# Weight-gradient products over 448 features as three full contractions and one half, with the halves of two output tiles on two row groups of the array

## The chip, the cores and the metric

The kernel runs on one core of one Trainium2 chip. The metric is device time in microseconds (us). Times from several runs are medians. TensorE multiplies and leaves its sums in PSUM, a memory that the kernel uses in banks of 512 columns. DVE (VectorE) and ACT (ScalarE) do elementwise work and copy the finished sums out of PSUM, POOL (GpSimd) does small copies, and SP issues the DMA transfers. PE is TensorE's row in the profile and PEld its weight loads, which put a stationary tile into the array; the granted clock is the share of its full clock that TensorE got.

## The reference, cut to what matters

The reference is forward and backward of a small network on one sequence of 2048 positions and 448 features: a spectral mixer (two-dimensional FFT, pointwise product with `A_w`, inverse FFT), then a token MLP of width 1792, each behind LayerNorms, with residuals. Eight outputs come back. Two of them matter here, the gradients of the MLP weights:

```
grad B_w1 (2048 x 1792) = LayerNorm(h)  (2048 x 448)  times  du        (448 x 1792)
grad B_w2 (1792 x 2048) = gelu(u)       (1792 x 448)  times  grad_out^T (448 x 2048)
```

Both contract over 448 features. No matmul in these kernels contracts more than 128 rows at a time, and 448 is 3.5 times 128.

## The kernel before

It contracts 448 as four times 112 (`DC = 112`). Activations are kept in blocks of 128 columns of which 112 are used, so that one DMA transpose makes four stationary tiles. The products are a generator. Each `yield` is one filler step. The other stages of the backward pass call `fill(n)` to put products between their own matmuls.

```python
RESH_LAG = 1.1
N_FILL_B = (16, 16, 40, 8, 32, 12)      # [2] before, [3] in, [4] after the spectral stage; [5] per inverse row

    rS = region("rS", 2 * NFB * 256)    # 7168 columns, scratch of the spectral stage
    ...
    def mm(out, lhsT, rhs, start, stop):
        nc.tensor.matmul(out, lhsT=lhsT, rhs=rhs, start=start, stop=stop)
    ...
    def gw_gen(n, rhs, width, store):
        for j in range(n):
            st = ahead.pop(0)                       # a transposed tile, 4 x 112 rows
            o = ost.next()
            for c in range(4):
                w = min(512, width - 512 * c)
                pw = ps_mm()                        # one of four PSUM banks
                for k in range(4):
                    mm(pw[:, 0:w], lhsT=st[0:DC, k, :], rhs=rhs(c, k), start=(k == 0), stop=(k == 3))
                    if k == 3:
                        evac(out=o[:, c * 512:c * 512 + w], in_=pw[:, 0:w])
                        if c == 3:
                            st_load()               # ask for a later transposed tile
                            defer(1.5, lambda j=j, o=o: store(j, o), o)
                    yield
    ...
    # the spectral stage on DVE, for two groups at a time
    ve.tensor_tensor(out=p1, in0=xc, in1=wr, op=ALU.mult)
    ve.tensor_tensor(out=p2, in0=xc, in1=wi, op=ALU.mult)
    ve.tensor_tensor(out=y[:, :, 1, :], in0=p1[:, :, 0, :], in1=p2[:, :, 1, :], ...)
    ve.tensor_tensor(out=y[:, :, 0, :], in0=p1[:, :, 1, :], in1=p2[:, :, 0, :], ...)
    # p1, p2, y and the emptied PSUM of the stage all lie in rS
```

Of the kernel before, what the change touches and what calls it, by code (L numbers as in the profile page):

```python
# [13 lines left out]
ALU = mybir.AluOpType  # L14
# [104 lines left out]
def kernel(  # L119
# [34 lines left out]
    def region(name, n):  # L154
        return mem.tile([P, n], BF16, name=name)
# [72 lines left out]
    r3 = region("r3", NG * 2 * KW)  # L228
    rS = region("rS", 2 * NFB * 256)
    rO = region("rO", 3 * S)  # L230
    rX = region("rX", NG * 2 * KW)
    r452 = region("r452", 8 * 452)
    rAT = region("rAT", 2 * 4 * P)
    rst = region("rst", 3 * 4 * P)
    r448 = region("r448", 8 * D)
# [21 lines left out]
    go_tp = cut(rC, 0, NT, D)  # L257
    dgu = cut(rD, 0, NFB, 4, P)[:, :, :, 0:DC]
    goT = cut(rG, 0, 4, S)
# [57 lines left out]
    gp_.memset(gtail, 0.0)  # L317
    nc.sync.dma_start(out=gtail[:, 0:DC], in_=grad_out[0][S - 16:S, 3 * DC:D])

# [462 lines left out]
    def dg_gen():  # L782
        for j in range(NFB):
            wT = w2Ts.pop(0)
            pg = ps_mm()
            for t in range(NT):
                mm(pg[:, 0:D], lhsT=wT[:, t, :], rhs=go_tp[:, t, :], start=(t == 0), stop=(t == NT - 1))
                if t == NT - 1:
                    evac(out=dgu[:, j, :, :], in_=v4(pg[:, 0:D]))
                    if w2T_ring.i >= cap[0]:  # L790
                        held_w2.append(load_w2T)
                    else:
                        load_w2T()
                yield
# [119 lines left out]
    hn = xn  # L914
    hln = cut(rB, 0, NT, 4, P)[:, :, :, 0:DC]

# [25 lines left out]
    def norm_h(t, on_act=False):  # L942
        if on_act:
            sc.activation(out=hln[:, t, :, :], in_=v4(hn[:, t, :]), func=ACT.Identity,
                          scale=rstd_h[:, t:t + 1], bias=nmr_h[:, t:t + 1])
        else:
            ve.tensor_scalar(out=hln[:, t, :, :], in0=v4(hn[:, t, :]), scalar1=nmean_h[:, t:t + 1],
                             scalar2=rstd_h[:, t:t + 1], op0=ALU.add, op1=ALU.mult)

    w2c_ring = Ring([cut(r, o, NFB, 256) for r, o in ((rS, 0), (rS, NFB * 256), (r452, 0), (rA, 0), (rA, NFB * 256), (r2, 0))])  # L950
# [18 lines left out]

    g_ = cut(rE, 0, NFB, 4, P)[:, :, :, 0:DC]  # L970
    gel = [ring(rG, i * 4 * 896, 4, 2, D) for i in range(2)]
# [27 lines left out]
    for jp in range(NFB // 2):  # L999
# [7 lines left out]
        for jj, ta, tb in spans:  # L1007
            fb = f0 + jj
            pu = pus[jj]
            for t in range(ta, tb):  # L1010
                mm(pu[:, 0:D], lhsT=w1c[:, t, jj * P:(jj + 1) * P], rhs=hln[:, t, :, :],
                                 start=(t == 0), stop=(t == NT - 1))
            if tb == NT:
                sc.activation(out=uf[:, jj, :], in_=pu[:, 0:D], func=ACT.Identity, bias=b1col[:, fb:fb + 1], scale=1.0)
        if jp + 3 < NFB // 2:
            w1cs.append(load_w1c(jp + 3))
        for fn in after_u.get(jp, ()):
            fn()
        gj = g_[:, f0:f0 + 2, :, :]

        def q4(ap):
            return ap.rearrange("p j (b c) -> p j b c", b=4)
        sc.activation(out=x2, in_=uf, func=ACT.Square)
# [4 lines left out]
        ve.tensor_scalar(out=hh, in0=z, scalar1=0.5, scalar2=0.5, op0=ALU.mult, op1=ALU.add)  # L1028
        ve.tensor_tensor(out=gj, in0=q4(uf), in1=q4(hh), op=ALU.mult)
        d = Later(ve, om_ops) if jp >= NFB // 2 - 2 else ve  # L1030
        d.tensor_scalar(out=om, in0=z, scalar1=-1.0, scalar2=1.0, op0=ALU.mult, op1=ALU.add)
        d.tensor_tensor(out=om, in0=om, in1=x2, op=ALU.mult)
        d.tensor_tensor(out=q4(om), in0=q4(om), in1=gj, op=ALU.mult)
        d.tensor_tensor(out=om, in0=om, in1=hh, op=ALU.add)
        for jj in range(2):
            d.tensor_tensor_reduce(out=dgu[:, f0 + jj, :, :], in0=dgu[:, f0 + jj, :, :], in1=v4(om[:, jj, :]), scale=1.0,
                                    scalar=0.0, op0=ALU.mult, op1=ALU.add, accum_out=gb1[:, f0 + jj:f0 + jj + 1])
    du = dgu
    gp_.memset(gb1b, 0.0)
# [6 lines left out]

    def load_goT(c):
        if c < 3:
            nc.sync.dma_start_transpose(out=goT[:, c, :], in_=grad_out[0][:, c * DC:c * DC + P])
            return  # L1050
        g0 = grad_out[0]
        nc.sync.dma_start_transpose(out=goT[:, 3, 0:S - 16],
                                    in_=bass.AP(g0.tensor, g0.offset + 3 * DC, [[D, S - 16], [1, P]]))
        nc.sync.dma_start_transpose(out=goT[:, 3, S - 16:S], in_=gtail)


    def y_head(t, lo_, hi_, py):
        for j in range(lo_, hi_):
            mm(py[:, 0:D], lhsT=w2cs[t // 2][:, j, (t % 2) * P:(t % 2 + 1) * P], rhs=g_[:, j, :, :],
                             start=(j == 0), stop=(j == NFB - 1))  # L1060
# [32 lines left out]
    ve.tensor_copy(out=gb2b[:], in_=gb2[:])  # L1093
    zero = mem.tile([P, P - DC], BF16, name="zero")
    gp_.tensor_scalar(out=zero[:], in0=gb2b[:], scalar1=0.0, scalar2=None, op0=ALU.mult)
    for reg, n in ((rE, NFB), (rD, NFB), (rB, NT)):
        gp_.tensor_copy(out=cut(reg, 0, n, 4, P)[:, :, :, DC:P].rearrange("p a b c -> p (a b) c"),
                        in_=zero[:, None, :].broadcast_to([P, 4 * n, P - DC]))
    defer(4.0, lambda: nc.sync.dma_start(out=out_7.rearrange("(p t) -> p t", t=NT), in_=gb2b[:]))
# [10 lines left out]
    def ln_bwd(t, i, ps, pscale, nrm, m2scale, rstd, resid, out):  # L1110
        pb, junk, tmp = m448.next(), m448.next(), m448.next()
        four = len(nrm.shape) == 3
        w = v4 if four else (lambda a: a)
        ms, m1, m2 = (lcol[:, i, k:k + 1] for k in range(3))
        sc.activation(out=pb, in_=ps, func=ACT.Identity, scale=pscale, accum_out=ms)
        ve.tensor_tensor_reduce(out=w(junk), in0=w(pb), in1=nrm, scale=m2scale, scalar=0.0,
                                op0=ALU.mult, op1=ALU.add, accum_out=m2)
        ve.tensor_scalar(out=m1, in0=ms, scalar1=1.0 / D, scalar2=None, op0=ALU.mult)
        ve.tensor_scalar(out=w(tmp), in0=nrm, scalar1=m2, scalar2=m1, op0=ALU.mult, op1=ALU.add)
        ve.tensor_tensor(out=pb, in0=pb, in1=tmp, op=ALU.subtract)  # L1120
        ve.scalar_tensor_tensor(out=out, in0=pb, scalar=rstd, in1=resid, op0=ALU.mult, op1=ALU.add)

    LAG = 3
    st_ring = ring(rst, 0, 3, 4, P)
    order = [(rE, j) for j in range(NFB)] + [(rB, t) for t in range(NT)]
    ahead = []

    def st_load():
        if order:
            reg, j = order.pop(0)  # L1130
            st = st_ring.next()
            nc.sync.dma_start_transpose(out=st, in_=reg[:, j * 512:(j + 1) * 512])
            ahead.append(st)
# [9 lines left out]
    for t in range(NT):  # L1143
        wT = w1Ts.pop(0)
        pdh = ps_mm()
        for j in range(NFB):
            mm(pdh[:, 0:D], lhsT=wT[:, j, :], rhs=du[:, j, :, :], start=(j == 0), stop=(j == NFB - 1))
        if t + 4 < NT:
            load_w1T(t + 4)
        ln_bwd(t, t, pdh[:, 0:D], 1.0, hln[:, t, :, :], (1.0 + LN_EPS) / D, rstd_h[:, t:t + 1], go_pt[:, t, :], dh[:, t, :])  # L1150
        if t % 2:
            fold_prep(dh, t // 2)
        if t >= NT - 3:
            st_load()
# [22 lines left out]

    ost = ring(rO, 0, 3, S)
    o4 = out_4.rearrange("(p t) f -> p t f", t=NT)

    def gw_gen(n, rhs, width, store):
        for j in range(n):
            st = ahead.pop(0)
            o = ost.next()
            for c in range(4):
                w = min(512, width - 512 * c)
                pw = ps_mm()
                for k in range(4):
                    mm(pw[:, 0:w], lhsT=st[0:DC, k, :], rhs=rhs(c, k), start=(k == 0), stop=(k == 3))
                    if k == 3:  # L1190
                        evac(out=o[:, c * 512:c * 512 + w], in_=pw[:, 0:w])
                        if c == 3:
                            st_load()
                            defer(1.5, lambda j=j, o=o: store(j, o), o)
                    yield

    pending.append(gw_gen(NFB, lambda c, k: goT[0:DC, k, c * 512:(c + 1) * 512], S,
                          lambda j, o: nc.sync.dma_start(out=out_6[j * P:(j + 1) * P, :], in_=o)))
    pending.append(gw_gen(NT, lambda c, k: du_t[0:DC, 4 * c:min(NFB, 4 * c + 4), k, :], F,
                          lambda t, o: nc.sync.dma_start(out=o4[:, t, :], in_=o[:, 0:F])))  # L1200
    nc.sync.dma_start(out=rC[:, 0:NG * 2 * KW], in_=w_d[:])
# [52 lines left out]
```

## Time and profile before

| | before |
|---|---|
| time, median | 388.18 us (386.99 to 388.26, 3 runs) |
| profiled execution | 386.6 us, granted clock 0.999 |
| product matmuls | 480 of 112 rows, 416 of 512 columns and 64 of 256 |

The busy time of each engine, from the first part of the profile page of the kernel before:

```profile
PE 353.7 (91%) x2089; PEld 192.4 (50%) x2089; DVE 286.2 (74%) x738; ACT 207.0 (54%) x437; POOL 24.0 (6%) x96
```

The table of windows gives the busy time by stage. The stretches below are the forward spectral stage (52 to 87.5), then in the backward pass the row transforms among which the products begin (244.1), the spectral stage, the filler after it, the inverse rows, and what follows the last inverse row. The columns are the stretch, its length, busy us (and instructions) of PE, PEld, DVE, ACT and POOL, the granted clock, the mean busy share of the DMA engines, and GB/s.

```profile
52.10:87.50 35.40, 30.22 (x184) 16.73 (x182) 29.17 (x67) 24.03 (x48) 0.96 (x3) 1.00 0.76 149
244.10:261.30 17.20, 15.69 (x92) 8.19 (x90) 9.49 (x19) 7.46 (x14) 0.00 (x0) 1.00 0.91 242
261.30:309.50 48.20, 46.14 (x233) 22.43 (x232) 45.38 (x94) 25.86 (x53) 0.00 (x0) 1.00 0.74 201
309.50:317.90 8.40, 8.40 (x43) 4.05 (x42) 3.56 (x6) 3.49 (x6) 0.00 (x0) 1.00 0.84 233
317.90:375.70 57.80, 52.69 (x321) 28.88 (x320) 43.02 (x114) 38.74 (x85) 0.00 (x0) 1.00 0.94 214
375.70:386.60 10.90, 6.84 (x38) 3.52 (x36) 5.39 (x12) 4.00 (x9) 0.00 (x0) 0.96 0.50 191
```

In the spectral stage TensorE and DVE are both nearly full. In the inverse rows TensorE idles 57.8 - 52.7 = 5.1 us, while the DMA engines are 94% busy. The list of waits for the inverse rows (who waited for what: us in total, times, longest) says what for:

```profile
DVE r L78 <- DMA out_dram<-r: 9.2, 5, 3.1
PE ps_mm L213 <- DVE rO L78: 3.6, 3, 2.1
PE ps_mm L213 <- DMA rst<-rB: 1.5, 1, 1.5
```

DVE wants to reuse a buffer whose row of `grad A_x` has not yet landed in DRAM. It is then late with emptying a PSUM bank, and TensorE waits for that. The timeline of TensorE shows the pace (start, length, operation, how many) and the end of the kernel:

```profile
268.17 1.89 PE L213 MATMUL ps_mm<-rG,rst 112*128 112x512 bf16 x8
...
372.53 2.75 PE L213 MATMUL ps_mm<-r,rst 112*128 112x512 bf16 x12
375.12 0.92 PE L213 MATMUL ps_ff<-csI,rAT 113*128 113x448 bf16 x4
375.88 6.66 PE L213 MATMUL ps_mm<-r,rst 112*128 112x256 bf16 x36
```

A run of eight lasts 1.89 us because the last one's pipeline is counted in; the starts are 0.216 us apart. After the last inverse row (375.12) 36 product matmuls are left, and they run while DVE and ACT finish the last LayerNorm.

### The profile page before, as it was taken

The numbers are of one execution on the slowest core, as the hardware profiler recorded it, in microseconds if no ns is written. First come the engines' busy times: TensorE is split into PE (matmuls) and PEld (weight loads), VectorE is DVE, ScalarE is ACT, GpSimd is POOL, SyncE is SP. The second block draws the span as 40 slices with busy tenths as digits, with TensorE's granted clock in tenths as the row PEclk, the third lists the DMA queues.
The fourth block names the chain that finished last, engine by engine and source line by source line (L and its number), as shares of the span: only waits on it lengthen the run. The fifth ranks groups of instructions, "written<-read, shape, count | busy, mean of one in ns | idle before, by whom it ended". The sixth has DMA issues, their size and how long they took to land.

```text
span 386.6 us, 6229 instructions
## 1 busy us (share of the span) xinstructions
PE 353.7 (91%) x2089; PEld 192.4 (50%) x2089; DVE 286.2 (74%) x738; ACT 207.0 (54%) x437; POOL 24.0 (6%) x96
## 2 busy tenths in 40 slices
PE   0888998789999999999999999899999899779995
PEld 0454655345645555555555666545544355445552
DVE  8999649973867887762269878738999945589694
ACT  4576646665966535233213444435545547557862
POOL 8600000000210000000030000000000000000000
PEclk9999999999999999999999999999999999999999
DMA  8999899537999999987857794595679889986994
GB/s 219 299 169 251 143 189 185 127 96 258 292 302 341 325 293 233 232 245 176 210 122 156 166 191 98 171 279 166 191 219 209 212 245 286 209 182 177 218 222 166
DMA packets 146248, 81.85 MB, mean 212 GB/s; under 512 B 97448, under 2 KB 140456, under 8 KB 145832
## 3 DMA queue, kind: packets, MB, share of 16 engines
q1 hardware_dynamic: 146216, 81.46, 86.6%
q8 instruction: 16, 0.26, 0.3%
q14 instruction: 16, 0.13, 0.1%
HBM read 27.56 MB, written 23.89 MB: 133 GB/s over the span
## 4 chain that ended last, share of the span: by engine, by line
PE 58%; DVE 26%; DMA 6%; ACT 4%; issue 4%; SPq 1%; POOL 0%; DVEq 0%; ACTq 0%; POOLq 0%
PE ps_mm L213 50%; DVE rS L78 10%; PE ps_ff L213 8%; DMA out_dram<-r 6%; DVE r L78 5%; DVE stats L78 2%; DVE rO L78 2%; ACT rO L78 2%; DVE rG L78 1%; DVE rX L78 1%; ACT rS L78 1%; DVE rC L78 1%; DVE rA L78 1%; DVE rD L78 1%; ACT csI L78 1%
## 5 line engine op out<-in xcount | busy, mean ns | idle before, releaser
L213 PEld LDWEIGHTS <-r 128*128 128x128 bf16 (+1 forms) x568 | 54.4, 105 | 43.6 <-issue 1.6
L213 PEld LDWEIGHTS <-rst 112*128 112x128 bf16 x480 | 45.9, 97 | 50.5 <-issue 5.7
L213 PE MATMUL ps_mm<-r,rst 112*128 112x512 bf16 (+1 forms) x256 | 52.0, 352 | 5.1 <-DVE rO L78 3.6
L213 PE MATMUL ps_mm<-rG,rst 112*128 112x512 bf16 x224 | 53.1, 378 | 0.0
L78 ACT CAST rO<-ps_mm 128x512 bf16<-128x512 f32 (+1 forms) x63 | 35.6, 572 | 31.9 <-PE ps_mm L213 30.4
L213 PEld LDWEIGHTS <-rS 128*128 128x128 bf16 (+1 forms) x368 | 32.0, 98 | 36.6 <-DVE rS L78 9.6
L78 DVE CAST rO<-ps_mm 128x512 bf16<-128x512 f32 (+1 forms) x57 | 35.1, 629 | 14.7 <-PE ps_mm L213 13.5
L213 PE MATMUL ps_mm<-rD,r 128*128 128x448 bf16 x224 | 44.5, 352 | 0.0
L213 PE MATMUL ps_mm<-rC,rE 128*128 128x448 bf16 x144 | 35.6, 367 | 1.5 <-DMA rE<-in_B_w_dram 1.5
L213 PE MATMUL ps_mm<-rB,r 128*128 128x448 bf16 x160 | 31.1, 352 | 0.1
L78 ACT CAST r<-ps_ff 128x452 bf16<-128x452 f32 x49 | 26.4, 540 | 6.5 <-PE ps_ff L213 6.5
L78 DVE SCALAR_TENSOR_TENSOR r<-ps_mm,b2col,r 128x448 bf16<-128x448 f32 x16 | 10.9, 683 | 20.2 <-PE ps_mm L213 18.2
L213 PE MATMUL ps_ff<-csI,rAT 113*128 113x448 bf16 x108 | 24.9, 353 | 0.4 <-ACT rAT L78 0.2
L78 ACT ACTIVATE r<-ps_mm 128x448 bf16<-128x448 f32 x16 | 8.7, 544 | 30.7 <-PE ps_mm L213 30.7
L78 ACT ACTIVATE r<-rC 128x448 bf16<-128x448 bf16 x16 | 9.1, 571 | 26.7 <-DMA out_dram<-r 13.5
L78 ACT ACTIVATE rS<-rS 128x452 bf16<-128x452 bf16 x16 | 9.3, 580 | 23.6 <-DVE rS L78 23.6
L213 PE MATMUL ps_mm<-rE,rS 128*128 128x448 bf16 x112 | 21.5, 352 | 0.0
L78 ACT ACTIVATE rG<-rG 128x896 bf16<-128x896 bf16 x14 | 13.3, 950 | 14.9 <-DVE rG L78 14.7
L213 PEld LDWEIGHTS <-rO 128*128 128x128 bf16 (+1 forms) x165 | 15.6, 98 | 10.6 <-ACT rO L78 0.2
L213 PEld LDWEIGHTS <-rE 128*128 128x128 bf16 x144 | 13.9, 101 | 12.1 <-DMA rE<-in_B_w_dram 1.9
L213 PE MATMUL ps_mm<-rC,rO 128*128 128x448 bf16 x80 | 18.9, 352 | 0.0
L78 ACT CAST rS<-ps_ff 128x512 bf16<-128x512 f32 x27 | 15.7, 586 | 5.4 <-PE ps_ff L213 5.4
(160 smaller groups left out, 573.0 us busy)
## 6 DMA issues: line engine op xcount, KB each, us to landing
out_dram<-rO SPq DMA_DIRECT2D x14, 512.0 KB
out_dram<-rO SPq DMA_DIRECT2D x16, 448.0 KB
r<-in_B_w_dram SPq DMA_DIRECT2D x5, 1024.0 KB
r<-r SPq DMA_DIRECT2D x16, 226.0 KB
r<-r SPq DMA_DIRECT2D x32, 113.0 KB
rS<-in_B_w_dram SPq DMA_DIRECT2D x4, 896.0 KB
out_dram<-r SPq DMA_DIRECT2D x32, 112.0 KB
rO<-in_B_w_dram SPq DMA_DIRECT2D x2, 1024.0 KB
```

What stands on the lines that cost most here:

```text
L78: fn(**kw)
L213: nc.tensor.matmul(out, lhsT=lhsT, rhs=rhs, start=start, stop=stop)
```

## The change

The intent is to save one eighth of the product matmuls' time. 448 rows become three full tiles of 128 and one half of 64. Two output tiles are made together. Their halves stand in rows 0 to 63 and 64 to 127 of one stationary block, so they can run on two row groups of the array at once. The Trainium skill ("TensorE: Matmul & The Clock Gate", Part 3) describes such tiles as running concurrently. To make one transposed tile of seven blocks, the last 64 features of the odd tile are copied in front of it, and the moving operands carry their last 64 features twice. The 112-of-128 layouts become dense ones.

```diff
-    rS = region("rS", 2 * NFB * 256)
+    rS = region("rS", 7232)
...
-    st_ring = ring(rst, 0, 3, 4, P)
-    order = [(rE, j) for j in range(NFB)] + [(rB, t) for t in range(NT)]
+    st_ring = Ring(ring(rst, 0, 2, 7, P).views + [cut(rS, 6336, 7, P)])
+    fold_ring.views.pop()
+    order = [(rE, j) for j in range(NFB // 2)] + [(rB, t) for t in range(NT // 2)]
...
-            nc.sync.dma_start_transpose(out=st, in_=reg[:, j * 512:(j + 1) * 512])
+            nc.sync.dma_start_transpose(out=st, in_=reg[:, j * 1024 + 64:j * 1024 + 960])
...
+        for u in range(n // 2):
+            def whole(pw, w, c, i, k, start, stop):
+                mm(pw[i][:, 0:w], lhsT=st[:, 4 * i + k, :], rhs=rhs(c, k, 0, P), start=start, stop=stop)
+            def parts(pw, w, c, start):
+                for i in range(2):
+                    mm(pw[i][:, 0:w], lhsT=st[64 * i:64 * i + 64, 3, :], rhs=rhs(c, 3, 64 * i, 64 * i + 64),
+                       start=start, stop=not start)
...
+            for c in range(0, 4, 2):
...
+                pw = [ps_mm(), ps_mm()]
+                for i in range(2):
+                    for k in range(3):
+                        whole(pw, 512, c, i, k, k == 0, False)
+                        yield
...
+                pv = [ps_mm(), ps_mm()]
+                parts(pw, 512, c, False)          # ends the two sums of chunk c
+                parts(pv, w, c + 1, True)         # begins the two sums of chunk c + 1
+                for i in range(2):
+                    out(pw, 512, c, i)
+                yield
+                yield
+                for i in range(2):
+                    for k in range(3):
+                        whole(pv, w, c + 1, i, k, False, k == 2)
+                        if k == 2:
+                            out(pv, w, c + 1, i)  # each half row is stored by itself
+                        yield
```

Cut here: POOL's zero-fill of the padding, which goes, the small POOL copies of 64 columns that replace it, the store buffers (six half rows instead of three rows), the number of transposed loads asked for in advance (two instead of three), and the renaming of layouts. The fill counts `N_FILL_B` stay as they are.

More of the change, by code (lines that the diff above doesn't have):

```diff
@@ L233 @@
     rAT = region("rAT", 2 * 4 * P)
-    rst = region("rst", 3 * 4 * P)
+    rst = region("rst", 2 * 7 * P)
     r448 = region("r448", 8 * D)
@@ L257 @@
     go_tp = cut(rC, 0, NT, D)
-    dgu = cut(rD, 0, NFB, 4, P)[:, :, :, 0:DC]
+    dgu = cut(rD, 0, NFB, 512)[:, :, 0:D]
     goT = cut(rG, 0, 4, S)
@@ L317 @@
     gp_.memset(gtail, 0.0)
-    nc.sync.dma_start(out=gtail[:, 0:DC], in_=grad_out[0][S - 16:S, 3 * DC:D])
+    nc.sync.dma_start(out=gtail[:, 0:64], in_=grad_out[0][S - 16:S, 3 * P:D])
     s896, s128, s2048 = _sin_scale(896), _sin_scale(128), _sin_scale(2048)
@@ L788, in dg_gen @@
                 if t == NT - 1:
-                    evac(out=dgu[:, j, :, :], in_=v4(pg[:, 0:D]))
+                    evac(out=dgu[:, j, :], in_=pg[:, 0:D])
                     if w2T_ring.i >= cap[0]:
@@ L914 @@
     hn = xn
-    hln = cut(rB, 0, NT, 4, P)[:, :, :, 0:DC]
+    hln = cut(rB, 0, NT, 512)[:, :, 64:512]
     hsum = mvh[:, :, 0]
@@ L943, in norm_h @@
         if on_act:
-            sc.activation(out=hln[:, t, :, :], in_=v4(hn[:, t, :]), func=ACT.Identity,
+            sc.activation(out=hln[:, t, :], in_=hn[:, t, :], func=ACT.Identity,
                           scale=rstd_h[:, t:t + 1], bias=nmr_h[:, t:t + 1])
         else:
-            ve.tensor_scalar(out=hln[:, t, :, :], in0=v4(hn[:, t, :]), scalar1=nmean_h[:, t:t + 1],
+            ve.tensor_scalar(out=hln[:, t, :], in0=hn[:, t, :], scalar1=nmean_h[:, t:t + 1],
                              scalar2=rstd_h[:, t:t + 1], op0=ALU.add, op1=ALU.mult)
+        if t % 2:
+            gp_.tensor_copy(out=rB[:, 512 * t:512 * t + 64], in_=rB[:, 512 * t + 448:512 * t + 512])
     w2c_ring = Ring([cut(r, o, NFB, 256) for r, o in ((rS, 0), (rS, NFB * 256), (r452, 0), (rA, 0), (rA, NFB * 256), (r2, 0))])
@@ L968 @@
     nc.sync.dma_start(out=h_d.rearrange("(p t) d -> p t d", t=NT), in_=hn)
-    g_ = cut(rE, 0, NFB, 4, P)[:, :, :, 0:DC]
+    g_ = cut(rE, 0, NFB, 512)[:, :, 64:512]
     gel = [ring(rG, i * 4 * 896, 4, 2, D) for i in range(2)]
@@ L1010 @@
             for t in range(ta, tb):
-                mm(pu[:, 0:D], lhsT=w1c[:, t, jj * P:(jj + 1) * P], rhs=hln[:, t, :, :],
+                mm(pu[:, 0:D], lhsT=w1c[:, t, jj * P:(jj + 1) * P], rhs=hln[:, t, :],
                                  start=(t == 0), stop=(t == NT - 1))
@@ L1018 @@
             fn()
-        gj = g_[:, f0:f0 + 2, :, :]
-        def q4(ap):
-            return ap.rearrange("p j (b c) -> p j b c", b=4)
+        gj = g_[:, f0:f0 + 2, :]
         sc.activation(out=x2, in_=uf, func=ACT.Square)
@@ L1028 @@
         ve.tensor_scalar(out=hh, in0=z, scalar1=0.5, scalar2=0.5, op0=ALU.mult, op1=ALU.add)
-        ve.tensor_tensor(out=gj, in0=q4(uf), in1=q4(hh), op=ALU.mult)
+        ve.tensor_tensor(out=gj, in0=uf, in1=hh, op=ALU.mult)
+        o1 = 512 * (f0 + 1)
+        gp_.tensor_copy(out=rE[:, o1:o1 + 64], in_=rE[:, o1 + 448:o1 + 512])
         d = Later(ve, om_ops) if jp >= NFB // 2 - 2 else ve
@@ L1032 @@
         d.tensor_tensor(out=om, in0=om, in1=x2, op=ALU.mult)
-        d.tensor_tensor(out=q4(om), in0=q4(om), in1=gj, op=ALU.mult)
+        d.tensor_tensor(out=om, in0=om, in1=gj, op=ALU.mult)
         d.tensor_tensor(out=om, in0=om, in1=hh, op=ALU.add)
         for jj in range(2):
-            d.tensor_tensor_reduce(out=dgu[:, f0 + jj, :, :], in0=dgu[:, f0 + jj, :, :], in1=v4(om[:, jj, :]), scale=1.0,
+            d.tensor_tensor_reduce(out=dgu[:, f0 + jj, :], in0=dgu[:, f0 + jj, :], in1=om[:, jj, :], scale=1.0,
                                     scalar=0.0, op0=ALU.mult, op1=ALU.add, accum_out=gb1[:, f0 + jj:f0 + jj + 1])
+            o1 = 512 * (f0 + jj)
+            dup = Later(gp_, om_ops) if d is not ve else gp_
+            dup.tensor_copy(out=rD[:, o1 + 448:o1 + 512], in_=rD[:, o1 + 384:o1 + 448])
     du = dgu
@@ L1047, in load_goT @@
     def load_goT(c):
+        g0 = grad_out[0]
         if c < 3:
-            nc.sync.dma_start_transpose(out=goT[:, c, :], in_=grad_out[0][:, c * DC:c * DC + P])
+            nc.sync.dma_start_transpose(out=goT[:, c, :], in_=g0[:, c * P:(c + 1) * P])
             return
-        g0 = grad_out[0]
         nc.sync.dma_start_transpose(out=goT[:, 3, 0:S - 16],
-                                    in_=bass.AP(g0.tensor, g0.offset + 3 * DC, [[D, S - 16], [1, P]]))
+                                    in_=bass.AP(g0.tensor, g0.offset + 3 * P, [[D, S - 16], [1, P]]))
         nc.sync.dma_start_transpose(out=goT[:, 3, S - 16:S], in_=gtail)
+        nc.sync.dma_start(out=goT[64:P, 3, :], in_=goT[0:64, 3, :])
     def y_head(t, lo_, hi_, py):
         for j in range(lo_, hi_):
-            mm(py[:, 0:D], lhsT=w2cs[t // 2][:, j, (t % 2) * P:(t % 2 + 1) * P], rhs=g_[:, j, :, :],
+            mm(py[:, 0:D], lhsT=w2cs[t // 2][:, j, (t % 2) * P:(t % 2 + 1) * P], rhs=g_[:, j, :],
                              start=(j == 0), stop=(j == NFB - 1))
@@ L1093 @@
     ve.tensor_copy(out=gb2b[:], in_=gb2[:])
-    zero = mem.tile([P, P - DC], BF16, name="zero")
-    gp_.tensor_scalar(out=zero[:], in0=gb2b[:], scalar1=0.0, scalar2=None, op0=ALU.mult)
-    for reg, n in ((rE, NFB), (rD, NFB), (rB, NT)):
-        gp_.tensor_copy(out=cut(reg, 0, n, 4, P)[:, :, :, DC:P].rearrange("p a b c -> p (a b) c"),
-                        in_=zero[:, None, :].broadcast_to([P, 4 * n, P - DC]))
     defer(4.0, lambda: nc.sync.dma_start(out=out_7.rearrange("(p t) -> p t", t=NT), in_=gb2b[:]))
@@ L1111, in ln_bwd @@
         pb, junk, tmp = m448.next(), m448.next(), m448.next()
-        four = len(nrm.shape) == 3
-        w = v4 if four else (lambda a: a)
         ms, m1, m2 = (lcol[:, i, k:k + 1] for k in range(3))
         sc.activation(out=pb, in_=ps, func=ACT.Identity, scale=pscale, accum_out=ms)
-        ve.tensor_tensor_reduce(out=w(junk), in0=w(pb), in1=nrm, scale=m2scale, scalar=0.0,
+        ve.tensor_tensor_reduce(out=junk, in0=pb, in1=nrm, scale=m2scale, scalar=0.0,
                                 op0=ALU.mult, op1=ALU.add, accum_out=m2)
         ve.tensor_scalar(out=m1, in0=ms, scalar1=1.0 / D, scalar2=None, op0=ALU.mult)
-        ve.tensor_scalar(out=w(tmp), in0=nrm, scalar1=m2, scalar2=m1, op0=ALU.mult, op1=ALU.add)
+        ve.tensor_scalar(out=tmp, in0=nrm, scalar1=m2, scalar2=m1, op0=ALU.mult, op1=ALU.add)
         ve.tensor_tensor(out=pb, in0=pb, in1=tmp, op=ALU.subtract)
@@ L1146 @@
         for j in range(NFB):
-            mm(pdh[:, 0:D], lhsT=wT[:, j, :], rhs=du[:, j, :, :], start=(j == 0), stop=(j == NFB - 1))
+            mm(pdh[:, 0:D], lhsT=wT[:, j, :], rhs=du[:, j, :], start=(j == 0), stop=(j == NFB - 1))
         if t + 4 < NT:
             load_w1T(t + 4)
-        ln_bwd(t, t, pdh[:, 0:D], 1.0, hln[:, t, :, :], (1.0 + LN_EPS) / D, rstd_h[:, t:t + 1], go_pt[:, t, :], dh[:, t, :])
+        ln_bwd(t, t, pdh[:, 0:D], 1.0, hln[:, t, :], (1.0 + LN_EPS) / D, rstd_h[:, t:t + 1], go_pt[:, t, :], dh[:, t, :])
         if t % 2:
             fold_prep(dh, t // 2)
-        if t >= NT - 3:
+        if t >= NT - 2:
             st_load()
@@ L1176, in bwd_mult @@
         return y
-    ost = ring(rO, 0, 3, S)
+    ost = ring(rO, 0, 6, S // 2)
     o4 = out_4.rearrange("(p t) f -> p t f", t=NT)
     def gw_gen(n, rhs, width, store):
-        for j in range(n):
+        for u in range(n // 2):
             st = ahead.pop(0)
-            o = ost.next()
-            for c in range(4):
-                w = min(512, width - 512 * c)
-                pw = ps_mm()
-                for k in range(4):
-                    mm(pw[:, 0:w], lhsT=st[0:DC, k, :], rhs=rhs(c, k), start=(k == 0), stop=(k == 3))
-                    if k == 3:
-                        evac(out=o[:, c * 512:c * 512 + w], in_=pw[:, 0:w])
-                        if c == 3:
-                            st_load()
-                            defer(1.5, lambda j=j, o=o: store(j, o), o)
-                    yield
@@ L1197 @@
-    pending.append(gw_gen(NFB, lambda c, k: goT[0:DC, k, c * 512:(c + 1) * 512], S,
-                          lambda j, o: nc.sync.dma_start(out=out_6[j * P:(j + 1) * P, :], in_=o)))
-    pending.append(gw_gen(NT, lambda c, k: du_t[0:DC, 4 * c:min(NFB, 4 * c + 4), k, :], F,
-                          lambda t, o: nc.sync.dma_start(out=o4[:, t, :], in_=o[:, 0:F])))
+            def whole(pw, w, c, i, k, start, stop):
+                mm(pw[i][:, 0:w], lhsT=st[:, 4 * i + k, :], rhs=rhs(c, k, 0, P), start=start, stop=stop)
@@ new lines, in parts, with out @@
+            def parts(pw, w, c, start):
+                for i in range(2):
+                    mm(pw[i][:, 0:w], lhsT=st[64 * i:64 * i + 64, 3, :], rhs=rhs(c, 3, 64 * i, 64 * i + 64),
+                       start=start, stop=not start)
+            def out(pw, w, c, i):
+                o = os_[i]
+                x = c % 2 * 512
+                evac(out=o[:, x:x + w], in_=pw[i][:, 0:w])
+                if x:
+                    if c == 3 and i:
+                        st_load()
+                    defer(1.5, lambda j=2 * u + i: store(j, 512 * (c - 1), x + w, o), o)
@@ new lines, in gw_gen @@
+            for c in range(0, 4, 2):
+                os_ = [ost.next(), ost.next()]
+                pw = [ps_mm(), ps_mm()]
[3 more added lines that the diff above has]
+                        yield
+                w = min(512, width - 512 * (c + 1))
+                pv = [ps_mm(), ps_mm()]
[11 more added lines that the diff above has]
+                        yield
@@ L1201 @@
+    pending.append(gw_gen(NFB, lambda c, k, a, b: goT[a:b, k, c * 512:(c + 1) * 512], S,
+                          lambda j, a, n, o: nc.sync.dma_start(out=out_6[j * P:(j + 1) * P, a:a + n], in_=o[:, 0:n])))
+    pending.append(gw_gen(NT, lambda c, k, a, b: du_t[a:b, 4 * c:min(NFB, 4 * c + 4), k, :], F,
+                          lambda t, a, n, o: nc.sync.dma_start(out=o4[:, t, a:a + n], in_=o[:, 0:n])))
     nc.sync.dma_start(out=rC[:, 0:NG * 2 * KW], in_=w_d[:])
```

## The prediction

> **What bounds it now.** The profile's first part has TensorE busy 91% of a 386.6 us span (DVE 74%, ACT 54%), at full clock. The products that change start at 244 us. The table of windows gives the stages. The spectral stage, 265 to 308 us, is bound by DVE and TensorE together: DVE is busy 9.7 to 9.8 of every 10 us from 270 to 310; an iteration takes 5.0 to 5.6 us. The inverse-row stage, 318 to 376 us, is bound by TensorE at 3.15 us an iteration, with some 5 us of gaps from 331 to 348 us, where DVE waited for output transfers (9.2 us in 5 waits) and TensorE for a transposed tile and for evictions. At the end, 36 product matmuls (375.9 to 382.5 us) hide the last LayerNorm work; then 4 us of eviction and store.
>
> **What is removed.** 480 product matmuls of 112 rows become 360 of 128 rows and 120 of 64. The timeline spaces 512-column matmuls by 0.216 us. If the halves run in pairs at once, 60 slots go: 12.1 us, counting the 256-column ones. The zero-fill on POOL goes too (3.6 us, hidden).
>
> **What is added.** 30 blocks of four half matmuls between full-array ones, so 60 switches of array mode. The Trainium skill, "TensorEngine Tiling (Array Packing)", Key Properties, says that a change of mode drains the array and that tiles work in parallel; no trace here has shown either. My estimate from this trace: a matmul lasts 379 ns against 216 spacing, so a drain costs up to 163 ns, and the weight load after it (98 ns) may be partly uncovered: 80 to 250 ns a switch. Block: 0.43 + 0.16 to 0.50 us, against 0.86 now. Net TensorE saving: 12.1 minus 5 to 15; I take 4. Evictions stay at 120. POOL's small copies lie off the chain; dense instead of 4x112 layouts gain nothing. Stores are twice as many, half as large; transposed loads move 13,440 instead of 15,360 columns.
>
> **How much is critical.** In the spectral stage DVE's own work does not shrink, and 16 fill steps now carry 18.3 matmuls, so it gets perhaps 1 to 4 us longer: accumulators finish two at a time, and a bank is wanted again after 6 matmuls rather than 12, so TensorE may wait for DVE's evictions. More products are then done there, and the gain appears in the inverse rows. The filler has 420 steps instead of 480, with unchanged fill counts: 168 steps remain for the inverse rows at 12 each, so the last two iterations have no filler. They run at the speed of ACT and DVE (about 2.3 us of DVE each), and the last LayerNorm tail and store are exposed: about 4 us lost against the present ending. Sum: -4 + 4, and 1 us less from lighter transfers and a smaller last store.
>
> **Prediction.** 387.0 us, 380 to 395 eight times in ten. Faster by over 2%: 0.10; within 2%: 0.80; slower by over 2%: 0.10.
>
> **What would show it.** Concurrency: start times of two halves within some 60 ns; a block of four taking 0.6 to 0.9 us. Spectral stage: 43 us or longer. End: two inverse-row iterations without product matmuls, TensorE mostly idle in the last 8 to 10 us. Everything before 244 us unchanged within 1 us.
>
> **What would make it wrong.** Halves that do not overlap: 7 to 15 us slower. Switches that cost almost nothing: up to 8 us faster. PSUM banks freed late, or transposed tiles of 896 columns, asked for one pair ahead, arriving late between 320 and 350 us: several us slower.

## The result and the profile after

The changed kernel took 382.92 us (median of 4 runs, 382.45 to 383.19) against 387.80 us for the kernel before in the same rounds. The ratio is 0.9875, with a 95% interval of 0.9854 to 0.9897. A ratio is the mean time of one kernel's fast runs over that of the other's of the same rounds, so it is not quite the ratio of the medians. The 1.25% are clear of the noise. Medians of different jobs come from different chips, so the comparisons below go by ratios.

The busy times of the changed kernel, from its profile page (span 381.4 us):

```profile
PE 348.6 (91%) x2089; PEld 181.7 (48%) x2089; DVE 284.7 (75%) x736; ACT 207.4 (54%) x439; POOL 29.0 (8%) x121
```

Its table of windows, for the same six stages:

```profile
51.60:85.90 34.30, 30.10 (x184) 16.63 (x182) 28.43 (x67) 24.00 (x48) 1.12 (x3) 1.00 0.78 152
242.40:260.50 18.10, 16.59 (x100) 7.59 (x98) 10.33 (x20) 7.91 (x15) 0.00 (x0) 1.00 0.91 258
260.50:310.60 50.10, 48.56 (x255) 20.69 (x254) 45.94 (x94) 29.25 (x57) 0.00 (x0) 1.00 0.79 208
310.60:318.70 8.10, 8.10 (x49) 3.54 (x48) 3.41 (x6) 3.09 (x7) 0.00 (x0) 1.00 0.83 234
318.70:372.90 54.20, 51.85 (x321) 24.90 (x319) 42.06 (x107) 38.00 (x86) 0.00 (x0) 1.00 0.88 224
372.90:381.40 8.50, 0.39 (x3) 0.00 (x0) 5.41 (x15) 1.87 (x6) 0.00 (x0) 0.74 0.20 71
```

Row by row against the kernel before: the products begin 1.7 us earlier (242.4 against 244.1), of which 1.1 us lie in the forward spectral stage, where the change seems to have nothing to do. The row transforms take 0.9 us longer, the spectral stage 1.9 us longer, the filler after it 0.3 us less, the inverse rows 3.6 us less, and the end 2.4 us less. The sum is -5.2 us, which is the difference of the two spans.

TensorE's busy time fell by 5.1 us, and its idle time stayed the same in sum (32.9 and 32.8 us). It moved: 2.8 us less in the inverse rows (57.8 - 52.69 against 54.2 - 51.85), 4.1 us more at the end (10.9 - 6.84 against 8.5 - 0.39).

A block of halves, in a narrow stretch of TensorE's timeline of the changed kernel:

```profile
265.28 0.26 PE L213 MATMUL ps_ff<-r,Ut 128*128 128x226 bf16 x1
265.47 0.39 PE L213 MATMUL ps_mm<-rG,rS 64*128 64x512 bf16 x2
```

In this stretch, which ends at 265.475, both halves of a pair have already started. The starts in the trace, read one by one, in us (the second column is the distance in ns from the start before):

```
265.276    full, 226 columns
265.468  192  half, rows 0-63      (226 columns alone would need 97)
265.472    4  half, rows 64-127
265.694  222  half, rows 0-63
265.698    4  half, rows 64-127
266.007  309  full, 512 columns    (512 columns alone need 216)
```

Over the 30 blocks the median cost of entering, beyond the spacing that the matmul in front has without a switch, is 96 ns, and of leaving 92 ns. Without waits a block of four halves of 512 columns lasts 538 ns from its first start to the next full one. So the halves do run at once, 3 or 4 ns apart, which agrees with the skill ("TensorE: Matmul & The Clock Gate", Part 3: about 4 ns). The change of mode that the skill says drains the array ("TensorEngine Tiling (Array Packing)", "Key Properties") costs about 0.1 us each way. Between full matmuls a weight load starts 214 ns before its own matmul; at a switch it starts only 4 ns before. The next start on the same rows is then 226 ns on instead of 216, so nearly all of the 0.1 us is a wait in front of the load, and hardly any of it the load itself, which lasts 93 to 96 ns. The 30 blocks give 12.1 us of matmul time and take 30 x 0.188 = 5.6 us back: 6.5 us net. (The expectation of run no_switch, quoted below, has 193 ns and 5.8 us; the spacing of 216 ns in the trace gives 188.) In 8 of the 30 blocks the second pair had to wait for its PSUM banks, 5.3 us in all (the expectation of run mm5, quoted below, says 9; a recount gives 8).

The waits in the inverse rows, after:

```profile
DVE r L78 <- DMA out_dram<-r: 2.2, 2, 1.6
PE ps_mm L213 <- ACT rO L78: 1.8, 4, 0.6
PE ps_mm L213 <- DVE rO L78: 0.3, 1, 0.3
```

DVE hardly waits for output transfers any more, though the core moved nearly the same bytes (81.63 against 81.85 MB). The end of TensorE's timeline has two inverse rows without product matmuls, and nothing behind the last:

```profile
368.18 2.22 PE L213 MATMUL ps_mm<-r,rS 128*128 128x512 bf16 x14
370.24 0.92 PE L213 MATMUL ps_ff<-csI,rAT 113*128 113x448 bf16 x4
371.00 0.39 PE L213 MATMUL ps_ff<-RTm,r 128*113 128x128 bf16 x4
371.22 0.92 PE L213 MATMUL ps_ff<-csI,rAT 113*128 113x448 bf16 x4
372.36 0.93 PE L213 MATMUL ps_ff<-csI,rAT 113*128 113x448 bf16 x4 [0.22 <-ACT rAT L78]
```

### The profile page after: what moved, and what is told of

It reads as the page before. It is cut to its first block, busy times and chain, and to the rows that moved or that the text cites. A ratio compares the mean times of both kernels' runs of the same rounds, so it can differ in the third digit from the quotient of the medians.

```text
span 381.4 us, 6293 instructions
## 1 busy us (share of the span) xinstructions
PE 348.6 (91%) x2089; PEld 181.7 (48%) x2089; DVE 284.7 (75%) x736; ACT 207.4 (54%) x439; POOL 29.0 (8%) x121
## 2 busy tenths in 40 slices
DMA packets 148249, 81.63 MB, mean 214 GB/s; under 512 B 95544, under 2 KB 140600, under 8 KB 147832
## 5 line engine op out<-in xcount | busy, mean ns | idle before, releaser
L213 PEld LDWEIGHTS <-rS 128*128 128x128 bf16 (+2 forms) x528 | 43.9, 98 | 54.2 <-issue 11.9
L78 ACT CAST rO<-ps_mm 128x512 bf16<-128x512 f32 (+1 forms) x64 | 34.5, 557 | 24.0 <-PE ps_mm L213 22.5
L213 PEld LDWEIGHTS <-rst 128*128 128x128 bf16 (+1 forms) x320 | 24.0, 97 | 36.3 <-issue 17.9
L213 PE MATMUL ps_mm<-rG,rst 128*128 128x512 bf16 (+1 forms) x160 | 36.1, 380 | 0.7 <-ACT rO L78 0.5
L78 ACT CAST r<-ps_ff 128x452 bf16<-128x452 f32 x53 | 28.4, 537 | 11.0 <-PE ps_ff L213 10.7
L213 PE MATMUL ps_mm<-r,rst 128*128 128x512 bf16 (+3 forms) x160 | 31.4, 353 | 2.3 <-ACT rO L78 2.3
L78 DVE SCALAR_TENSOR_TENSOR r<-ps_mm,b2col,r 128x448 bf16<-128x448 f32 x16 | 10.9, 683 | 20.0 <-PE ps_mm L213 18.3
L213 PE MATMUL ps_mm<-r,rS 128*128 128x512 bf16 (+3 forms) x96 | 18.7, 354 | 0.6 <-DVE rO L78 0.3
L78 DVE TENSOR_SCALAR rG<-rG 128x896 bf16<-128x896 bf16 x28 | 11.0, 394 | 10.2 <-ACT rG L78 10.1
```

Source lines behind the costliest of these rows:

```text
L78: fn(**kw)
```

## The experiments

Twelve kernels ran, in three jobs, each on one chip. All were timed in five rounds.

| run | median us | ratio to before | 95% interval |
|---|---|---|---|
| the change | 382.92 | 0.9875 | 0.9854 to 0.9897 |
| full_halves (wrong) | 385.28 | 0.9927 | 0.9902 to 0.9952 |
| same_group (wrong) | 389.97 | 1.0059 | 1.0030 to 1.0087 |
| no_switch (wrong) | 383.27 | 0.9870 | 0.9844 to 0.9895 |
| mm5 | 381.94 | 0.9842 | 0.9817 to 0.9868 |
| before_halfstore | 389.26 | 1.0035 | 1.0003 to 1.0068 |
| light_store (incomplete) | 382.64 | 0.9870 | 0.9839 to 0.9901 |
| no_switch_light (wrong) | 376.00 | 0.9702 | 0.9675 to 0.9728 |
| fill_s7 | 384.19 | 0.9909 | 0.9881 to 0.9938 |
| before_rs | 385.01 | 0.9957 | 0.9938 to 0.9976 |
| after_rs | 386.19 | 0.9988 | 0.9967 to 1.0010 |
| before_light (incomplete) | 381.57 | 0.9864 | 0.9842 to 0.9886 |
| mm5_i11 | 381.69 | 0.9867 | 0.9846 to 0.9889 |

The kernel before took 388.1, 387.36 and 386.84 us (medians of 11 runs each) in the three jobs.

### full_halves: the change without row tiles

```diff
-                    mm(pw[i][:, 0:w], lhsT=st[64 * i:64 * i + 64, 3, :], rhs=rhs(c, 3, 64 * i, 64 * i + 64),
-                       start=start, stop=not start)
+                    mm(pw[i][:, 0:w], lhsT=st[:, 3, :], rhs=rhs(c, 3, 0, P),
+                       start=start, stop=not start)
```

> The changed kernel with its four half matmuls of a block made full ones of 128 rows (results of these products wrong on purpose), so no row tiles and no switches; everything else of the change stays. Theory (row tiling itself brings the gain): the matmul slots come back, 22 blocks by 0.23 us and 8 by 0.12 us, about 6 us more TensorE time; 387 to 389 us, the gain over the kernel before gone. Rival (the gain is from lighter stores and transposed loads and the dense layout): 383 to 385 us, still faster than the kernel before by 3 us or more.

It came out between the two: 0.9927. With the matmul count of the kernel before, the change is still 0.7% (some 2.8 us) faster than it, and row tiles add about 0.5% (some 2 us), though they give back 6.5 us of matmul time. Neither theory holds alone. The gain beside row tiling had to be found, and also the place where two thirds of the 6.5 us went.

### same_group: halves that cannot run at once

```diff
+                    mm(pw[i][:, 0:w], lhsT=st[0:64, 3, :], rhs=rhs(c, 3, 0, 64),
+                       start=start, stop=not start)
```

> The changed kernel with both halves of a pair in rows 0 to 63 (results wrong on purpose): the mode switches stay, the two halves cannot run at once. Theory (concurrency of the halves pays for the switches): halves start 216 ns apart instead of 4, a block costs 1.06 us and not 0.64, 12 us more TensorE time in all, 391 to 396 us, slower than the kernel before. Rival (halves gain nothing from standing in different row groups): within 2 us of the changed kernel.

1.0059, slower than the kernel before: the concurrency is real and needed. The starts of the four halves stand 226, 216 and 216 ns apart, and the block lasts 966 ns instead of 538. Entering and leaving cost 96 and 92 ns, as before. The weight load of the second half was hidden behind the first half's matmul although both use the same rows: it starts 214 ns before its own matmul. The time was just below the expected range (389.97 us against 391 to 396): 1.8% over the change, some 7 us, for 12 us of added matmul time.

### no_switch: no change of array mode

```diff
+                    if i == 0:
+                        mm(pw[i][:, 0:w], lhsT=st[:, 3, :], rhs=rhs(c, 3, 0, P), start=start, stop=not start)
...
-                        whole(pw, 512, c, i, k, k == 0, False)
+                        whole(pw, 512, c, i, k, k == 0, i == 1 and k == 2)
...
-                        whole(pv, w, c + 1, i, k, False, k == 2)
+                        whole(pv, w, c + 1, i, k, i == 1 and k == 0, k == 2)
```

> The changed kernel with each block's four halves replaced by two full matmuls (results wrong on purpose): the same streaming time, no change of array mode. Theory: the 30 blocks lose the 193 ns of entry and exit measured in the trace, 5.8 us of TensorE time; most of it critical, so 377 to 380 us. Rival (switches are hidden behind DVE in the spectral stage and by bank waits): 381.5 to 383 us.

The theory failed: 0.9870, no faster than the change, with 5.6 us less to do on TensorE. The time, 383.27 us, is the rival's within 0.3 us, but the rival's reason, DVE and the banks, was not what the next two runs found. The waits in the inverse rows show what took the time:

```profile
DVE r L78 <- DMA out_dram<-r: 6.7, 3, 2.9
PE ps_mm L213 <- DVE rO L78: 6.6, 4, 2.2
```

The waits for output transfers are back, and with them TensorE's waits for DVE.

### light_store and no_switch_light: with most of the product stores taken away

```diff
-                          lambda j, a, n, o: nc.sync.dma_start(out=out_6[j * P:(j + 1) * P, a:a + n], in_=o[:, 0:n])))
+                          lambda j, a, n, o: nc.sync.dma_start(out=out_6[j * P:(j + 1) * P, a:a + 256], in_=o[:, 0:256])))
```

(The other product's store likewise; the same edit on top of no_switch makes no_switch_light.)

> The changed kernel storing only the first 256 columns of each half row of the products (outputs incomplete on purpose), which takes away some 10 MB of output transfers. Theory (with the switches removed the time did not fall, because transfers from 280 to 345 us set the pace): 377 to 380.5 us. Rival (eviction and LayerNorm work on DVE and ACT set the pace): 381.5 to 383.5 us.

> The kernel without mode switches (wrong on purpose), also storing only the first 256 columns of each half row. Theory (transfers hid the 5.6 us of switches): 4 us or more below the light-store run with switches, 372 to 376 us. Rival (DVE, ACT or bank turnover hide them): within 1.5 us of the light-store run with switches.

Lighter stores do nothing for the change (0.9870 against 0.9875): its pace is not set by the product stores. Without switches they are worth 1.7% (0.9702 against 0.9870), and of the two light kernels, timed in the same job, the one without switches is 6.6 us faster, as the theory of no_switch_light has it. So in the changed kernel TensorE sets the pace, and transfers stand close behind it. If the switches' 5.6 us are removed, the kernel runs into the transfers at once. Both theories of light_store were put too simply: each is right for one of the two kernels. The windows of no_switch and of no_switch_light for their inverse rows show it, 57.4 against 49.5 us, with the same matmuls:

```profile
316.40:373.80 57.40, 50.18 (x297) 27.11 (x295) 41.40 (x106) 37.70 (x87) 0.00 (x0) 0.97 0.88 210
```

```profile
316.10:365.60 49.50, 48.21 (x297) 26.57 (x296) 41.58 (x106) 38.04 (x87) 0.00 (x0) 1.00 0.75 158
```

### before_light: the same edit on the kernel before

```diff
-                          lambda j, o: nc.sync.dma_start(out=out_6[j * P:(j + 1) * P, :], in_=o)))
+                          lambda j, o: nc.sync.dma_start(out=out_6[j * P:(j + 1) * P, 0:512], in_=o[:, 0:512])))
```

> The kernel before storing only the first 512 columns of each product row (outputs incomplete on purpose). In its inverse rows TensorE idles 6.0 us and DVE waits 9 us for output transfers. Theory (these idle times come from the transfers): 382 to 385 us, DVE's waits for output transfers under 3 us. Rival (they come from order and bank turnover): 386.5 to 388.5 us. The changed kernel did not gain from lighter stores.

In time the theory holds, and by more than it said: 0.9864, some 5 us. DVE's waits for output transfers fell only from 9.2 to 4.1 us, though, and not under 3 us as expected. In the inverse rows TensorE's idle time falls from 5.1 us to 53.9 - 52.4 = 1.5 us:

```profile
317.80:371.70 53.90, 52.40 (x320) 28.93 (x319) 43.92 (x115) 38.84 (x85) 0.00 (x0) 1.00 0.73 160
371.70:380.00 8.30, 6.89 (x39) 3.52 (x36) 4.85 (x12) 4.04 (x9) 0.00 (x0) 1.00 0.23 77
```

```profile
DVE r L78 <- DMA out_dram<-r: 4.1, 4, 2.9
```

The kernel before thus lost about 5 us to its output transfers, and the change loses none that lighter stores would give back. The loss has two parts: of the 6.6 us between the two profiled executions, 3.9 lie in the inverse rows and 2.6 in the last stretch, where the store of the last product row, issued at 383.1 us, ends the kernel before. In the change the products end before the last inverse rows, so no product store stands at its end.

With light stores the two kernels are equal (0.9864 and 0.9870, in different jobs): where transfers do not bind, the saved matmul time is spent again. The spectral stage takes 50.4 us in light_store and 48.2 in before_light, and at the end TensorE idles 8.5 us against 1.4. The two last stretches of light_store:

```profile
319.40:372.20 52.80, 50.99 (x321) 24.83 (x320) 42.22 (x107) 38.12 (x86) 0.00 (x0) 1.00 0.65 150
372.20:381.10 8.90, 0.36 (x2) 0.00 (x0) 5.39 (x15) 1.84 (x6) 0.00 (x0) 0.78 0.14 48
```

### before_halfstore: is it the smaller stores?

```diff
-    ost = ring(rO, 0, 3, S)
+    ost = ring(rO, 0, 6, S // 2)
...
...
-                            defer(1.5, lambda j=j, o=o: store(j, o), o)
+                        if x:
+                            defer(1.5, lambda j=j, o=o, c=c, n=x + w: store(j, 512 * (c - 1), n, o), o)
```

> The kernel before with the product rows stored in two half rows each (256 KB instead of 512 KB a store), as the change does; nothing else changed. Making the halves full matmuls left the changed kernel 2.8 us faster than before, with the same matmul slots, so something beside row tiling gains. Theory (small stores let the LayerNorm outputs land sooner): 385 to 386.5 us, DVE's waits for output transfers in the inverse rows fall from 9 us to under 5 us. Rival (the gain is from fewer transposed loads or from the filler running out earlier): 387.5 to 389 us, waits as before.

No: 1.0035, if anything slower, and DVE's waits for output transfers stay at 8.6 us:

```profile
DVE r L78 <- DMA out_dram<-r: 8.6, 4, 3.4
```

The relief has another cause. full_halves has it too (2.5 us of DVE's waits, and 1.9 of ACT's), so row tiles are not needed for it. before_rs (below) keeps 8.8 us of the waits, and after_rs, with two buffers for the transposed tiles, has none, so neither the region's width nor the third buffer brings it. Two candidates that remain are the fewer and larger transposed loads and the quicker pace of the filler: 420 steps carry the work of the 480 matmuls, so more products are made and stored before the inverse rows begin. These two were not separated. The number of loads alone does not decide it: the kernel before issues 12 transposed loads in the inverse rows and the change 4, but no_switch, also with 4, waits 6.7 us. The cause of the relief stays open.

### before_rs and after_rs: the width of a scratch region

The forward spectral stage was 1.1 us shorter. The instructions and their durations there are the same, but one step differs: the first of two combining instructions. The timeline of DVE of the kernel before and of the changed one, for the same place:

```profile
82.67 0.82 DVE L78 TENSOR_TENSOR rS<-rS 128x452 bf16<-128x452 bf16 x2
83.53 1.17 DVE L78 TENSOR_TENSOR rS<-rX,rG 128x904 bf16<-128x904 bf16 x2
```

```profile
82.15 1.17 DVE L78 TENSOR_TENSOR rS<-rX,rG 128x904 bf16<-128x904 bf16 x2
83.42 0.70 DVE L78 TENSOR_TENSOR rS<-rS 128x452 bf16<-128x452 bf16 x2
```

The pair takes 0.82 us before and 0.70 after. The traces show why: before, the second of the pair waits for a semaphore of DVE itself, that is, for the first to have finished, and starts 430 ns after it. After, it does not, and starts 311 ns after it; the first lasts some 395 ns in both. The two write interleaved halves of one buffer and do not depend on each other. Changing the width of the region `rS` alone makes all 16 such waits disappear, one per step of the two spectral stages.

```diff
# before_rs, on the kernel before
-    rS = region("rS", 2 * NFB * 256)
+    rS = region("rS", 7232)

# after_rs, on the changed kernel
-    rS = region("rS", 7232)
+    rS = region("rS", 2 * NFB * 256)
-    st_ring = Ring(ring(rst, 0, 2, 7, P).views + [cut(rS, 6336, 7, P)])
+    st_ring = ring(rst, 0, 2, 7, P)
```

> The kernel before with one number changed: the scratch region of the spectral stage is 7232 columns wide instead of 7168, as in the change. The build then drops 16 waits of DVE on its own previous instruction, in the two spectral stages; in the traces the step after the first combining subtraction falls from 430 to 311 ns. Theory (half or more of what remained with full halves comes from this side effect): 16 steps of 0.12 us, 1.5 to 2.5 us less, 385 to 386.5 us, and the forward spectral stage 1.1 us shorter. Rival (the gain beside row tiling is in the transfers or the filler): within 0.7 us of the kernel before.

> The changed kernel with the scratch region back at 7168 columns (the transposed tiles then use two buffers instead of three), which brings the 16 self-waits of DVE back. Theory: 1.5 to 2.5 us slower than the changed kernel, 384.3 to 385.5 us. Rival: within 0.7 us of it.

The width alone makes the kernel before 0.4% faster (0.9957, some 1.7 us). The forward stage takes 34.3 us as in the change, against 35.4, and the backward spectral stage 47.6 against 48.2:

```profile
51.60:85.90 34.30, 30.06 (x184) 16.71 (x182) 28.45 (x67) 24.00 (x48) 0.86 (x3) 1.00 0.76 152
259.60:307.20 47.60, 45.81 (x233) 22.47 (x232) 44.93 (x94) 25.87 (x53) 0.00 (x0) 1.00 0.77 204
```

Its products begin at 242.4 us, as in the change, so no other part of the change is needed to explain the earlier start. (0.5 of the 1.7 us lie before the forward stage. It begins at 51.6 us in before_rs and in the change, but at 52.1 in full_halves, which has the width too, so this part is scatter.) Put back in the change, it costs more than expected: 0.9988 against 0.9875, 1.1% (the profiled executions differ by 2.6 us, 384.0 against 381.4). Of these 2.6 us, the forward stage again accounts for 1.1 and the backward spectral stage for 0.7. But after_rs also has two buffers for the transposed tiles instead of three, and it ran in another job than the change. How much of its loss is the waits alone stays open. The sign is clear in both. And with the width put back, row tiles and all, the change is no longer shown to be faster than the kernel before (0.9967 to 1.0010).

### mm5, fill_s7, mm5_i11: can the rest be had?

```diff
# mm5
-        return psum.tile([P, 512], F32, tag="ff", bufs=4, name="ps_ff")
+        return psum.tile([P, 512], F32, tag="ff", bufs=3, name="ps_ff")
-        return psum.tile([P, 512], F32, tag="mm", bufs=4, name="ps_mm")
+        return psum.tile([P, 512], F32, tag="mm", bufs=5, name="ps_mm")
# fill_s7
-N_FILL_B = (16, 16, 40, 8, 32, 12)
+N_FILL_B = (16, 16, 40, 7, 32, 12)
# mm5_i11: mm5, and
+N_FILL_B = (16, 16, 40, 8, 32, 11)
```

> The changed kernel with five PSUM banks for the products and three for the rest. In the changed kernel's trace 9 of 30 blocks wait inside the block, 5.3 us in all, for a bank that is not yet evicted. Theory (bank turnover limits part of the gain): these waits fall below 2 us and the time by 1 to 4 us, to 379 to 382 us. Rival (the waits only stand in for DVE and ACT being full): the waits move elsewhere, 382 to 384 us; three banks for the rest may cost 1 to 3 us in the row stages.

> The changed kernel with 7 filler steps instead of 8 after each half iteration of the spectral stage, so that the 420 steps last to the final inverse-row iteration. In the trace the spectral stage grew by 1.9 us and the PE idled 8 us at the end. Theory (the filler should be spread over the last iterations): the spectral stage gets 3 to 4 us shorter, the end keeps its filler, 379 to 382 us. Rival (total transfers or DVE work fix the end): 382.5 to 384.5 us.

> The changed kernel with five PSUM banks for the products and 11 filler steps instead of 12 in an inverse-row iteration, so that the filler lasts to the final iteration. Theory (TensorE's idle 8 us at the end can be used): 379.5 to 381.5 us. Rival (the sum of TensorE work and the last LayerNorm chain fix the end, as the run with 7 steps in the spectral stage suggests): 382 to 384 us.

With a fifth bank the waits inside the blocks fall from 5.3 to 1.3 us, as the theory has it. (A count that takes two missing matmul records for waits gives 1.8.) The spectral stage gets 0.9 us shorter. The time falls by 0.3% (0.9842 against 0.9875), and the intervals overlap, so it is not clear of the noise: DVE's waits for output transfers rise from 2.2 to 4.3 us, and the products begin 1.6 us later, of which 0.5 us lie in the forward spectral stage. Spreading the filler by taking it from the spectral stage did not help (0.9909): that stage got 2.7 us shorter and the inverse rows 4 us longer. mm5_i11 (0.9867) equals the change. In these two TensorE still idles 6.7 and 7.5 us after the last inverse row has begun (8.1 in the change), so the end was hardly filled, and what filling it would be worth stays open. mm5 has the lowest ratio of all correct kernels, but no version was shown to beat the change.

## Why the prediction was right or wrong, point by point

The measured time lies in the predicted range, and "within 2%" was the likely one. But the range is 15 us wide, so lying in it says little about the mechanism. The predicted gain was about 1 us and the measured one about 5, so several terms of the sum were off.

1. *"Halves that run in pairs at once ... 12.1 us"* was right: 3 to 4 ns apart.
2. *"80 to 250 ns a switch ... I take 4"*: the measured 96 and 92 ns lie in the range, near its low end. The prediction took a value nearer the middle, so the net is 6.5 us and not 4. This term was mis-sized by 2.5 us.
3. *"it gets perhaps 1 to 4 us longer"* for the spectral stage: 1.9 us, right. The reason given, banks wanted sooner, is seen in part: 8 of 30 blocks waited for a bank, three of them in this stage, 1.9 us in all. A fifth bank took these waits away and shortened the stage by 0.9 us (mm5), so they explain about half of it, as far as that run shows.
4. *"the last two iterations have no filler ... about 4 us lost"*: right as to TensorE's idle time. TensorE idles 8.1 us after the last inverse row began, against 4.1 us.
5. *"1 us less from lighter transfers and a smaller last store"* was the largest mistake. The kernel before loses about 5 us to transfers (before_light), and the changed one none that light stores give back (light_store). The prediction saw the 9.2 us of DVE's waits and the 5 us of TensorE's gaps, but let only 1 us of them go. What took them away in the change is not shown; the fewer, larger transposed loads and the quicker pace of the products are the candidates. Smaller stores did not (before_halfstore). The store of the last product row, too, no longer ends the kernel.
6. *"Everything before 244 us unchanged within 1 us"* was wrong: 1.7 us earlier. The step that failed is the reading of the diff's first line. A wider scratch region was taken for storage alone, and it took away 16 waits of DVE on itself. With that line alone the products begin the same 1.7 us earlier (before_rs), 0.5 us of which is scatter.

In short, row tiles free 6.5 us on TensorE. About 2 us of that reach the total with everything else of the change in place (full_halves against the change). The rest goes into the spectral stage, where TensorE and DVE are both busy over 90% of the time, and into the end, where the filler has run out. Of the other 0.7% of the gain, the dropped waits bring about 0.4% when they are dropped alone (before_rs). That the remaining 0.3% come from output transfers that no longer hold DVE up fits the waits but is not clear of the noise. These parts were measured in different jobs and do not add up: putting the width back in the change, with one buffer for transposed tiles fewer, cost the whole gain (after_rs).

## What to carry to other kernels

Saved matmul time counts only where nothing else is close to the limit. Before planning to save more of it, take away the transfers and see whether the time moves, as no_switch and no_switch_light did here. Halves on two row groups pay when several stand together: here one block of four halves needs 0.63 us with its switches, against 1.06 us for the same halves in the same rows and 4 x 0.216 = 0.86 us for four full matmuls. Compare the waits in the built program as well as the source; a buffer's size can add or remove them.

## What the Trainium skill lacked or had wrong

- "TensorEngine Tiling (Array Packing)", "Key Properties", says that a mode change drains the array but gives no cost. Measured here: 96 ns to enter and 92 ns to leave a block of 64-row matmuls, beyond the spacing of matmuls without a switch (medians over 30 blocks; 96 and 92 ns in same_group and mm5 too).
- "TensorE: Matmul & The Clock Gate", Part 3, "The mechanism", says in one line that weight loads overlap with running matmuls only when the row group differs. In same_group the halves used the same rows and still started 216 ns apart (226 the first time), so a 94 ns load was hidden. The same section also lets a load run ahead into a background weight buffer, which would fit; the line leaves that case out.
- The speedup table of the same Part 3 has no entry for two row tiles. Measured: four halves of 512 columns in 538 + 96 = 634 ns with both switches, against 966 + 96 = 1062 ns in one row group, a factor of 1.68.
- "VectorE: DVE Perf Modes", "The DRAIN you can't avoid", says of its row of eight copies that the semaphores between them cost nothing extra. Its first paragraph adds that an instruction that is not held starts earlier, but gives no time for it. Here an instruction that waits for DVE's own previous one starts 430 ns after it, and 311 ns after it when there is no such wait (128 partitions x 452 columns, bf16), so the wait costs 119 ns.
